# A block-causal attention with hashed experts: V fetched in two-token runs, interleaved key tiles, expert weights in 16 KB runs from batch 6 on

## The chip, the cores and the metric

One Trainium2 chip, of which the program uses one core. The metric is device microseconds of one execution, from the first to the last work of that core. Engines go by these names: PE (TensorE: PE for the matmul, PEld for the load of its stationary operand), DVE (VectorE), ACT (ScalarE), POOL (GpSimd), SP (SyncE, here only an issuer of transfers). "Lnnn" is a line of the kernel before.

## What is computed

Attention over 8 batches x 8 heads x 576 tokens x 64 dimensions in f32, causal in blocks of 64 tokens, then a mixture of experts in which a hash of the token's id, not its content, chooses one of 8 experts:

```python
scores = (1.0 / np.sqrt(D)) * np.matmul(q, k.transpose(0, 1, 3, 2))
mask = (pos[:, None] // 64) >= (pos[None, :] // 64)
attn = softmax(np.where(mask, scores, -1e9))          # rows
x = (attn @ v).transpose(0, 2, 1, 3).reshape(4608, 512)
e = token_ids * 2654435761 % 8
out[t] = np.maximum(x[t] @ w1[e[t]], 0.0) @ w2[e[t]]  # w1: 512x1024, w2: 1024x512, per expert
```

## The kernel before, in words

**Phase one, attention.** The order of the work is written out by hand: one loop over 32 head pairs (g = 4 b + pr: batch b, pair pr of two heads), plus two turns at the end, since PV lags two pairs behind. One turn issues, in this order: `S_chunk(g, 0)` and `S_chunk(g, 1)`, `PV(g-2, 0)`, the transposes `T_pair(g+1)` (and `T_rest` before a new batch), `S_chunk(g, 2)` (and `S_rest` in the first pair), `PV(g-2, 1)`; then the casts of the next batch and, between them, the loads of the one after that.

The first 512 tokens of a head are handled in four tiles of 128, the last 64 ("rest") by themselves. q and k are loaded with four neighbouring tokens per partition (1 KB runs; L106), the rest rows apart (L112). `cast_qk` turns them into bf16 on DVE (L169, L174), PE transposes them (L215), DVE copies the result to `qkT` (L220), and in this copy sorts the columns so that tile i holds tokens 128i to 128i+127. Within a tile the tokens stand in the order c, j for token 4j + c.

`S_chunk` (L245) makes scores with keys on partitions and queries on the free axis: three chunks of 2 heads x 512 columns into one of three `ps` buffers. `mm_pair` (L225) multiplies both heads, whose 64 dimensions lie on partitions 0 to 63 and 64 to 127 of the array. In a diagonal tile the upper 64 keys must not be seen by the lower 64 queries: two small matmuls (L239) of `maskk` and `maskq` add -30000 there. ACT takes the exponential of a whole chunk (L258) into `pt`. The rest rows get their own 64x64 scores (L266).

`PV` (L287) multiplies, for each head, 15 times (L299 x14, L304) into `O`, of which there is one buffer; a column of ones beside V gives the sum of each row. DVE takes the reciprocal (L309) and multiplies (L310) into the bf16 tile `xs`, 512 columns per token.

V is loaded with tokens matched to that order: 16 transfers of 64 KB per batch in runs of one token, 256 bytes (L122), and two for the rest (L128), all from SP's queue, in which q, k and V of batch after batch follow each other (`ld` has two buffers of each). `cast_v` on POOL (L179, L182) makes bf16 of it in `vx`, with two buffers.

`scatter_x(b-1)` on POOL (L323, in pair 1 of batch b) writes each token's row to the place in `x_dram` that `route()` has worked out (sorted by expert, 640 places per expert, on DVE during the first pairs of batch 0). Expert weights are cast from f32 to bf16 by the transfer itself, issued on POOL by `load_weights` (L471, L473) into one of three buffers: expert 0 in batch 3, expert 1 in batch 5, expert 2 in batch 7, always after that turn's scatter.

**Phase two, FFN.** When all rows are placed, SP issues the transposing load of expert 0's x (L553), the read of the rows' token numbers (L456), then the other experts' x. `stage_a` (L558) computes relu(x w1): per 128 columns of the hidden layer eight matmuls of 320 columns (L566), ACT does the relu (L571). `stage_b` (L576) multiplies by w2 (L581), DVE copies (L586), POOL scatters the rows to the output (L588). A loop over overflowing tiles follows (L614), which finds nothing to do here or little.

Of the kernel before, what the change touches and what calls it, by code (L numbers as in the profile page):

```python
# [14 lines left out]
ET = mybir.EngineType  # L15

# [4 lines left out]
NT = 4  # L21
# [13 lines left out]
def kernel(  # L35
# [27 lines left out]
    maskq = const.tile([P, 64], BF16, name="maskq")  # L63
# [14 lines left out]

    nc.vector.memset(maskk[:], 0.0)
    nc.vector.memset(maskq[:], 0.0)  # L80
    for m in range(2):
        nc.vector.memset(
            maskk[64 * m : 64 * m + 1, :].rearrange("p (c h j) -> p c h j", c=4, h=2)[:, :, 1, :], NEG)
        nc.vector.memset(maskq[64 * m : 64 * m + 1, :], 1.0)
# [32 lines left out]
    def load_v(b):  # L117
        vf = ld.tile([P, 36, D], F32, name="vf", tag="vf")
        vm = vf[:, 0:32, :].rearrange("p (h i) d -> p h i d", h=H)
        for i in range(NT):  # L120
            for c in range(4):
                nc.sync.dma_start(  # L122
                    vm[32 * c : 32 * c + 32, :, i, :],
                    v[b, :, 128 * i : 128 * i + 128, :].rearrange(
                        "h (j c) d -> c j h d", c=4)[c],
                )
        for m in range(2):
            nc.sync.dma_start(  # L128
                vf[64 * m : 64 * m + 64, 32:36, :],
                v[b, :, 512:576, :].rearrange("(r m) s d -> m s r d", m=2)[m],  # L130
            )
        loaded[b][2] = vf
# [3 lines left out]
    for z in range(2):  # L136
        vx = fix.tile([P, H, NT, D + 1], BF16, name=f"vx{z}")
        v4 = fix.tile([P, NP, 2, D + 1], BF16, name=f"v4{z}")
        nc.vector.memset(vx[:, :, :, D : D + 1], 1.0)
        nc.gpsimd.memset(v4[:], 0.0)  # L140
        for m in range(2):
            nc.vector.memset(v4[64 * m : 64 * m + 64, :, m, D : D + 1], 1.0)
        vexts.append((vx, v4))
# [32 lines left out]
    def cast_v(b):  # L176
        vf = loaded[b][2]
        vx, v4 = vexts[b % 2]
        nc.gpsimd.tensor_copy(  # L179
            vx[:, :, :, 0:D], vf[:, 0:32, :].rearrange("p (h i) d -> p h i d", h=H))  # L180
# [24 lines left out]
    def T_pair(g):  # L205
# [4 lines left out]
        tp = psT.tile([P, 8, P], BF16, name="tp", tag="tp")  # L210
        for w in range(2):
            src = casted[b][w]
            for c in range(4):
                s0 = (pr * 4 + c) * 2
                nc.tensor.transpose(  # L215
                    out=tp[:, 4 * w + c, :],
# [3 lines left out]
        nc.vector.tensor_copy(  # L220
            qk[:, pr, :, 0:512].rearrange("p w (i c j) -> p w c i j", i=4, c=4),
            tp[:].rearrange("p (w c) (i j) -> p w c i j", w=2, i=4),
        )

    def mm_pair(b, pr, ps, o0, i, q0, n):  # L225
        qk = qkTs[b]
        diag = q0 == 128 * i
        for m in range(2):
# [3 lines left out]
                lhsT=qk[rows, pr, 1, 128 * i : 128 * i + 128],  # L232
                rhs=qk[rows, pr, 0, q0 : q0 + n],
                start=True, stop=not diag,
            )
        if diag:
            for m in range(2):
                rows = slice(64 * m, 64 * m + 64)
                nc.tensor.matmul(  # L239
                    ps[:, m, o0 : o0 + 128].rearrange("p (c h j) -> p c h j", c=4, h=2)[:, :, 0, :],  # L240
                    lhsT=maskk[rows, :], rhs=maskq[rows, :].rearrange("p (c j) -> p c j", c=4),
                    start=False, stop=True,
                )

    def S_chunk(g, ch):  # L245
        b, pr = divmod(g, NP)
        ps = psS.tile([P, 2, 512], F32, name="ps", tag="ps")
        if ch == 0:
            mm_pair(b, pr, ps, 0, 0, 0, 512)
        elif ch == 1:  # L250
            mm_pair(b, pr, ps, 0, 1, 128, 448)
            mm_pair(b, pr, ps, 448, 0, 512, 64)
        else:
            mm_pair(b, pr, ps, 0, 2, 256, 320)
            mm_pair(b, pr, ps, 320, 3, 384, 192)
# [20 lines left out]
    def pt_off(i, q0):  # L276
        if i == 0:
            return q0 if q0 < 512 else 960
        if i == 1:
            return 512 + q0 - 128  # L280
        if i == 2:
            return 1024 + q0 - 256
        return 1344 + q0 - 384

    xss = {}

    def PV(g, m):  # L287
# [8 lines left out]
        for t in range(5):  # L296
            for i in range(min(t, NT - 1) + 1):
                o0 = m * PTW + pt_off(i, 128 * t)
                nc.tensor.matmul(  # L299
                    O[:, t, :], lhsT=pt[:, o0 : o0 + 128], rhs=vx[:, h, i, :],  # L300
                    start=(i == 0), stop=(i == t),
# [9 lines left out]
            out=xs[:, :, h * D : (h + 1) * D], in0=O[:, :, 0:D],  # L311
            in1=rs[:].to_broadcast([P, 5, D]), op=ALU.mult,
# [156 lines left out]
    def load_weights(e):  # L469
        w1b = wts.tile([P, DM // P, FF], BF16, name="w1b", tag="w1b")  # L470
        nc.gpsimd.dma_start(w1b[:], moe_w1[e].rearrange("(db p) f -> p db f", p=P))  # L471
        w2b = wts.tile([P, FF // P, DM], BF16, name="w2b", tag="w2b")
        nc.gpsimd.dma_start(w2b[:], moe_w2[e].rearrange("(fb p) o -> p fb o", p=P))  # L473
# [27 lines left out]
    for g in range(NPAIRS + 2):  # L501
# [29 lines left out]
        if pr == 1 and b >= 1:  # L531
            scatter_x(b - 1)
            if b == 3:
                load_weights(0)
            if b == 5:
                load_weights(1)
            if b == 7:
                load_weights(2)
# [19 lines left out]
    def stage_a(e):  # L558
# [3 lines left out]
        for ft in range(NFT):  # L562
            hp = psH.tile([P, 2, 512], F32, name="hp", tag="hp")
            for db in range(NKT):
                for t in range(2):
                    nc.tensor.matmul(  # L566
                        hp[:, t, 0:HC], lhsT=w1b[:, db, ft * P : (ft + 1) * P],
# [32 lines left out]
    load_x(1)  # L600
    hts = {}
# [12 lines left out]
    with tc.For_i(0, n_ov, 1) as j:  # L614
# [3 lines left out]
            w1b[:], moe_w1[bass.ds(eo, 1)].rearrange("e (db p) f -> p (e db) f", p=P))  # L618
        w2b = wts.tile([P, NFT, DM], BF16, name="w2b", tag="w2b")
        nc.gpsimd.dma_start(  # L620
            w2b[:], moe_w2[bass.ds(eo, 1)].rearrange("e (fb p) o -> p (e fb) o", p=P))
# [15 lines left out]
        for ft in range(NFT):  # L637
            hp = psY.tile([P, P], F32, name="hpo", tag="yp")
            for db in range(NKT):
                nc.tensor.matmul(hp[:], lhsT=w1b[:, db, ft * P : (ft + 1) * P], rhs=xt[:, db, :],  # L640
# [42 lines left out]
```

The softmax here doesn't subtract the row's maximum and nothing guards it: scores larger than these inputs give would overflow.

## Time and profile before

| What | us |
|---|---|
| median of 3 runs (lowest, highest) | 362.71 (361.36, 366.07) |
| the profiled execution / its span | 359.15 / 357.5 |
| attention: first scores, last O written out | 10.18, 190.2 |
| last scatter of x issued; first x transpose issued | 197.1; 200.97 |
| first and last FFN matmul's start | 205.64, 348 |
| busy: PE, ACT, DVE, POOL | 258.6, 143.5, 134.0, 126.5 |
| mean granted TensorE clock | 0.86 |

The profile cuts the span into 40 slices of 8.9 us and gives each engine's busy share in tenths; "PEclk" is the granted clock, "DMA" the share of the 16 DMA engines. The granted clock is 0.99 over the FFN phase and 0.68 to 0.92 over the batches of attention. Windows give busy microseconds (and instruction counts) in a stretch. In a list of waits the columns are: engine, line, what it waited for, microseconds in total, times, longest. In the order of time a line gives start, length, engine, line, tile written and read, count, and in brackets the idle time before it and who ended it. DMA volumes are counted as written, so a weight of 2 MB in f32 counts 1 MB. Other groups that matter: 96 exponentials of 1031 ns, 64 multiplies (L310) of 491, 8 casts of V (L179) of 1892, 16 of its rest (L182) of 399, 896 PV matmuls, 320 + 256 score and mask matmuls.

### The profile page before, as it was taken

Reading aid. Unit: us, or ns where it says so; the run is one execution under the profiler, and the core shown is the slowest. Engines: PE = TensorE matmul, PEld = TensorE weight load, DVE = VectorE, ACT = ScalarE, POOL = GpSimd, SP = SyncE. Lnnn points to the kernel's source line nnn. Section 1 sums busy time; section 2 is a strip of 40 time slices with the busy share of each in tenths; the row PEclk is TensorE's granted clock in tenths of the full one; section 3 lists DMA queues with packets and bytes.
Section 4 is the critical chain, followed back from the end, with each engine's and each line's share of the span. In section 5 each row is a group of like instructions: output and inputs, shape, how many; then the busy total and the mean of one; then the engine's idle time right before and its main releaser. Section 6 shows DMA issues by size and latency. Waiting matters only on the chain. (4 is left out here: it accounts for less than half of the span.)

```text
span 357.5 us, 6826 instructions
## 1 busy us (share of the span) xinstructions
PE 258.6 (72%) x2727; PEld 167.6 (47%) x2727; DVE 134.0 (37%) x311; ACT 143.5 (40%) x177; POOL 126.5 (35%) x154
## 2 busy tenths in 40 slices
PE   1425698496682776826961099999999989999990
PEld 0213475365462554624740067464747464646440
DVE  6528787454750756507551000213030303030330
ACT  1225397658291582913950046141515041415100
POOL 2040225726504556045374000343341606061451
PEclk9998599959586795865885579999999999999997
DMA  7678596879999989999149793469999998989231
GB/s 209 149 218 235 125 288 166 261 200 270 201 199 237 254 247 230 197 215 277 43 98 186 169 148 76 132 149 183 185 157 258 173 232 173 231 158 226 107 129 43
DMA packets 109152, 66.42 MB, mean 186 GB/s; under 512 B 75957, under 2 KB 101557, under 8 KB 109120
## 3 DMA queue, kind: packets, MB, share of 16 engines
q1 hardware_dynamic: 89984, 33.56, 40.7%
q0 software_dynamic: 17536, 31.24, 40.2%
q10 hardware_dynamic: 1600, 1.18, 1.1%
q8 instruction: 22, 0.36, 0.4%
q14 instruction: 10, 0.08, 0.1%
HBM read 61.92 MB, written 16.61 MB: 220 GB/s over the span
## 5 line engine op out<-in xcount | busy, mean ns | idle before, releaser
L258 ACT ACTIVATE pt<-ps 128x1024 bf16<-128x1024 f32 x96 | 92.1, 1031 | 81.1 <-PE ps L239 80.9
L571 ACT ACTIVATE hT<-hp 128x640 bf16<-128x640 f32 x64 | 45.0, 703 | 103.8 <-PE hp L566 103.8
L566 PE MATMUL hp<-xT,w1b 128*128 128x320 bf16 x512 | 72.7, 304 | 17.9 <-DMA xT<-x_dram 16.2
L299 PE MATMUL O<-vx,pt 128*128 128x65 bf16 x896 | 47.8, 214 | 42.5 <-DVE xs L310 27.4
L588 POOL DMA_INDIRECT out_dram<-ysb,perm x40 | 40.0, 999 | 104.5 <-DVE ysb L586 103.2
L581 PE MATMUL yp<-w2b,hT 128*128 128x512 bf16 x320 | 70.2, 379 | 0.0
L586 DVE COPY ysb<-yp 128x512 f32<-128x512 f32 x40 | 27.7, 691 | 112.1 <-PE yp L581 70.7
L566 PEld LDWEIGHTS <-w1b 128*128 128x128 bf16 x512 | 50.5, 99 | 40.3 <-issue 16.3
L299 PEld LDWEIGHTS <-pt 128*128 128x128 bf16 x896 | 39.4, 110 | 50.2 <-DVE xs L310 30.2
L323 POOL DMA_INDIRECT x_dram<-xs,slot_i x40 | 44.6, 1115 | 26.9 <-DVE xs L310 15.5
L581 PEld LDWEIGHTS <-hT 128*128 128x128 bf16 x320 | 31.3, 98 | 36.6
L179 POOL CAST vx<-vf 128x2048 bf16<-128x2048 f32 x8 | 15.1, 1892 | 90.5 <-DMA vf<-in_v_dram 79.3
L230 PE MATMUL ps<-qkT 64*128 64x512 bf16 (+4 forms) x320 | 44.5, 350 | 0.2
L310 DVE TENSOR_TENSOR xs<-O,rs 128x320 bf16<-128x320 f32 x64 | 31.4, 491 | 2.2
L230 PEld LDWEIGHTS <-qkT 64*128 64x128 bf16 x320 | 18.4, 106 | 20.0 <-issue 7.5
L239 PE MATMUL ps<-maskq,maskk 64*128 64x64 bf16 x256 | 25.5, 213 | 0.0
L309 DVE RECIPROCAL rs<-O 128x5 f32<-128x5 f32 x64 | 12.3, 192 | 31.1 <-PE O L304 30.6
L220 DVE COPY qkT<-tp 128x1024 bf16<-128x1024 bf16 x32 | 21.8, 682 | 4.1 <-PE tp L215 3.8
L169 DVE CAST qb<-qf 128x2048 bf16<-128x2048 f32 (+2 forms) x9 | 10.7, 1194 | 32.1 <-DMA qf<-in_q_dram 32.1
L215 PE MATMUL tp<-identbf,qb 128*128 128x128 bf16 x128 | 15.1, 253 | 9.5 <-DVE qb L169 9.5
L215 PE MATMUL tp<-identbf,kb 128*128 128x128 bf16 x128 | 14.8, 249 | 4.3 <-DVE kb L169 4.3
L215 PEld LDWEIGHTS <-qb 128*128 128x128 bf16 x128 | 9.6, 115 | 9.7 <-DVE qb L169 9.6
(99 smaller groups left out, 135.1 us busy)
## 6 DMA issues: line engine op xcount, KB each, us to landing
vf<-in_v_dram SPq DMA_DIRECT2D x144, 64.0 KB
w1b<-in_moe_w_dram POOLq DMA_DIRECT2D x8, 1024.0 KB, 8.0
w2b<-in_moe_w_dram POOLq DMA_DIRECT2D x8, 1024.0 KB, 14.8
qf<-in_q_dram SPq DMA_DIRECT2D x7, 1024.0 KB
kf<-in_k_dram SPq DMA_DIRECT2D x7, 1024.0 KB
x_dram<-zx SPq DMA_DIRECT2D x8, 136.0 KB
qf<-in_q_dram SPq DMA_DIRECT2D x16, 64.0 KB
kf<-in_k_dram SPq DMA_DIRECT2D x14, 64.0 KB
```

The lines of the kernel that those rows point to most:

```text
L215: nc.tensor.transpose(out=tp[:, 4 * w + c, :], in_=src[:, s0 : s0 + 2, :].rearrange("p a d -> p (a d)"), identity=identbf[:],)
L230: nc.tensor.matmul(ps[:, m, o0 : o0 + n], lhsT=qk[rows, pr, 1, 128 * i : 128 * i + 128], rhs=qk[rows, pr, 0, q0 : q0 + n], start=True, sto ...
L239: nc.tensor.matmul(ps[:, m, o0 : o0 + 128].rearrange("p (c h j) -> p c h j", c=4, h=2)[:, :, 0, :], lhsT=maskk[rows, :], rhs=maskq[rows, : ...
L258: nc.scalar.activation(ptv[:, :, 512 * ch : 512 * ch + 512], ps[:], ACT.Exp, scale=SCALE)
L299: nc.tensor.matmul(O[:, t, :], lhsT=pt[:, o0 : o0 + 128], rhs=vx[:, h, i, :], start=(i == 0), stop=(i == t),)
L310: nc.vector.tensor_tensor(out=xs[:, :, h * D : (h + 1) * D], in0=O[:, :, 0:D], in1=rs[:].to_broadcast([P, 5, D]), op=ALU.mult,)
L323: ins = nc.gpsimd.indirect_dma_start(out=x_dram[:, :], out_offset=bass.IndirectOffsetOnAxis(ap=slot_i[0:n, i, b : b + 1], axis=0), in_=xs[ ...
L566: nc.tensor.matmul(hp[:, t, 0:HC], lhsT=w1b[:, db, ft * P : (ft + 1) * P], rhs=xT[:, db, t * HC : (t + 1) * HC], start=(db == 0), stop=(db ...
L571: nc.scalar.activation(hT[:, ft, :].rearrange("p (t n) -> p t n", t=2), hp[:, :, 0:HC], ACT.Relu)
L581: nc.tensor.matmul(yp[:], lhsT=hT[:, ft, tt * P : (tt + 1) * P], rhs=w2b[:, ft, :], start=(ft == 0), stop=(ft == NFT - 1),)
L586: nc.vector.tensor_copy(ysb[:], yp[:])
L588: ins = nc.gpsimd.indirect_dma_start(out=out[:, :], out_offset=bass.IndirectOffsetOnAxis(ap=perm3[:, gg : gg + 1], axis=0), in_=ysb[:], in ...
```

## The change

- **V**: 8 transfers of 128 KB per batch instead of 16 of 64 KB. A run is two neighbouring tokens, 512 bytes. The 256 tokens 256r to 256r+255 now form two key tiles: even and odd tokens (slot 2r + c), instead of two tiles of 128 consecutive tokens.
- **Scores**: queries keep their four tiles. Key tiles of 256r.. now matter in part for a query tile: for query tiles 0 and 2 only the lower half of two key tiles is seen. These halves are put together into one 128-row piece by `mm_c`, with 64x64 pieces. The masks change with it, and a pair has 30 score and mask matmuls instead of 18. `T_pair` writes the transposes directly in the wanted order, so the copy to `qkT` is straight. The exponentials keep their number and size, and PV its 15 matmuls a head, from the columns that the table `PVS` lists.
- **cast_v**: `vx` has six slots instead of four; two more POOL copies bring the two lower halves together.
- **Weights**: row p of the array holds w1's rows 4p to 4p+3 and w2's rows 8p to 8p+7: 16 KB in one run for either. So the columns of x are permuted when `PV` writes `xs` (reading `O` with a step of four), and w1's stationary operand takes every eighth column.
- **When**: expert 0 in the first pair of batch 6 (ahead of the scatter of batch 5, which is issued a turn later), expert 1 in pair 1 of batch 7, expert 2 behind the first two x transposes in the program, so on POOL right after the last scatter.

```diff
     def load_v(b):
-        vm = vf[:, 0:32, :].rearrange("p (h i) d -> p h i d", h=H)
-        for i in range(NT):
-            for c in range(4):
-                nc.sync.dma_start(
-                    vm[32 * c : 32 * c + 32, :, i, :],
-                    v[b, :, 128 * i : 128 * i + 128, :].rearrange("h (j c) d -> c j h d", c=4)[c])
+        vm = vf[:, 0:32, :].rearrange("p (h r c) d -> p h r (c d)", h=H, r=2)
+        for r in range(2):
+            for hf in range(2):
+                for u in range(2):
+                    p0 = 64 * hf + 32 * u
+                    t0 = 256 * r + 128 * hf
+                    nc.sync.dma_start(
+                        vm[p0 : p0 + 32, :, r, :],
+                        v[b, :, t0 : t0 + 128, :].rearrange("h (j u c) d -> u j h (c d)", u=2, c=2)[u])
     def cast_v(b):
-        nc.gpsimd.tensor_copy(vx[:, :, :, 0:D], vf[:, 0:32, :].rearrange("p (h i) d -> p h i d", h=H))
+        vm = vf[:, 0:32, :].rearrange("p (h s) d -> p h s d", h=H)
+        nc.gpsimd.tensor_copy(vx[:, :, 0:4, 0:D], vm)
+        nc.gpsimd.tensor_copy(vx[0:64, :, 4:6, 0:D], vm[0:64, :, 0::2, :])
+        nc.gpsimd.tensor_copy(vx[64:128, :, 4:6, 0:D], vm[0:64, :, 1::2, :])
     def T_pair(g):
...
-                nc.tensor.transpose(out=tp[:, 4 * w + c, :], in_=..., identity=identbf[:])
-        nc.vector.tensor_copy(qk[:, pr, :, 0:512].rearrange("p w (i c j) -> p w c i j", i=4, c=4),
-                              tp[:].rearrange("p (w c) (i j) -> p w c i j", w=2, i=4))
+                if w == 0:
+                    o = tp[:, 0, :].rearrange("p (i c j) -> p c i j", i=4, c=4)[:, c]
+                else:
+                    o = tp[:, 1, :].rearrange("p (r x h u j) -> p u x r h j", r=2, x=2, h=2, u=2)[:, c // 2, c % 2]
+                nc.tensor.transpose(out=o, in_=..., identity=identbf[:])
+        nc.vector.tensor_copy(qk[:, pr, :, 0:512], tp[:])
+    def mm_c(b, pr, ps, o0, r):
+        for x in range(2):
+            for m in range(2):
+                rows = slice(64 * m, 64 * m + 64)
+                nc.tensor.matmul(ps[64 * x : 64 * x + 64, m, o0 : o0 + 128],
+                    lhsT=qk[rows, pr, 1, 256 * r + 128 * x : 256 * r + 128 * x + 64],
+                    rhs=qk[rows, pr, 0, 256 * r : 256 * r + 128], start=False, stop=False)
     def S_chunk(g, ch):
-        if ch == 0:
-            mm_pair(b, pr, ps, 0, 0, 0, 512)
-        elif ch == 1:
-            mm_pair(b, pr, ps, 0, 1, 128, 448)
-            mm_pair(b, pr, ps, 448, 0, 512, 64)
+        if ch < 2:
+            mm_pair(b, pr, ps, 0, ch, 128, 448, first=True)
+            mm_pair(b, pr, ps, 448, 3 - ch, 512, 64)
+            mm_mask(ps, 0, False, 1, last=True)
         else:
-            mm_pair(b, pr, ps, 0, 2, 256, 320)
-            mm_pair(b, pr, ps, 320, 3, 384, 192)
+            mm_pair(b, pr, ps, 256, 2, 384, 128, first=True)
+            mm_pair(b, pr, ps, 384, 3, 384, 128)
+            mm_mask(ps, 256, False, 2)
+            mm_c(b, pr, ps, 0, 0)
+            mm_c(b, pr, ps, 128, 1)
+            mm_mask(ps, 0, True, 2, last=True)
     def PV(g, m):
...
-            out=xs[:, :, h * D : (h + 1) * D], in0=O[:, :, 0:D],
-            in1=rs[:].to_broadcast([P, 5, D]), op=ALU.mult,
+            out=xs[:, :, 0:DM].rearrange("p t (d h k) -> p h t d k", d=4, h=H)[:, h],
+            in0=O[:, :, 0:D].rearrange("p t (k d) -> p t d k", d=4),
+            in1=rs[:, :, :, None].to_broadcast([P, 5, 4, D // 4]), op=ALU.mult,
     def load_weights(e):
-        nc.gpsimd.dma_start(w1b[:], moe_w1[e].rearrange("(db p) f -> p db f", p=P))
+        nc.gpsimd.dma_start(w1b[:], moe_w1[e].rearrange("(p db) f -> p db f", p=P))
-        nc.gpsimd.dma_start(w2b[:], moe_w2[e].rearrange("(fb p) o -> p fb o", p=P))
+        nc.gpsimd.dma_start(w2b[:], moe_w2[e].rearrange("(p fb) o -> p fb o", p=P))
     # the loop over pairs
         if pr == 1 and b >= 1:
             scatter_x(b - 1)
-            if b == 3: load_weights(0)
-            if b == 5: load_weights(1)
-            if b == 7: load_weights(2)
+            if b == 7: load_weights(1)
+        if pr == 0 and b == 6: load_weights(0)
     def stage_a(e):
-                        hp[:, t, 0:HC], lhsT=w1b[:, db, ft * P : (ft + 1) * P],
+                        hp[:, t, 0:HC], lhsT=w1b[:, db, ft::NFT],
     # ahead of the FFN loop
     load_x(0)
     read_perm()
     load_x(1)
+    load_weights(2)
```

## The prediction

> **What bounds the kernel now.** I read the page's slices first, then windows cut at each batch, then SP's queue in order of time, the DMA queues in single windows, the waits, and last the few microseconds in which nothing is short.
>
> The slices, and the busy times of one batch without and one with a weight fetch, and of the FFN phase (sum columns: PE, PEld, DVE, ACT, POOL, granted clock, DMA share, GB/s):
>
> ```profile
> PE   1425698496682776826961099999999989999990
> DMA  7678596879999989999149793469999998989231
> 72.90:92.66 19.76, 14.70 (x238) 10.92 (x236) 11.08 (x27) 12.17 (x15) 9.38 (x11) 0.76 0.88 238
> 92.66:115.48 22.82, 14.18 (x217) 10.48 (x213) 8.35 (x21) 11.25 (x13) 6.22 (x7) 0.72 0.99 198
> 205.64:348.70 143.06, 141.25 (x832) 81.81 (x832) 27.58 (x43) 44.99 (x64) 47.62 (x49) 0.99 0.85 170
> ```
>
> The FFN phase is TensorE's (141.25 of 143.06 us). Attention, from 10 to 190 us, is not: no engine passes 17 us of 20 while the DMA share is 0.88 to 0.99. What paces the transfers is SP's own queue:
>
> ```profile
> 62.48 0.56 SPq L106 DMA_DIRECT2D qf<-in_q_dram  x1
> 65.03 3.21 SPq L112 DMA_DIRECT2D kf<-in_k_dram  x2
> 68.34 10.91 SPq L122 DMA_DIRECT2D vf<-in_v_dram  x16
> 79.29 1.26 SPq L128 DMA_DIRECT2D vf<-in_v_dram  x2
> 80.65 0.55 SPq L106 DMA_DIRECT2D qf<-in_q_dram  x1
> 88.35 16.56 SPq L122 DMA_DIRECT2D vf<-in_v_dram  x16
> ```
>
> SP issues without a pause, q, k, then V, batch after batch; from one batch's q to the next 19.83, 18.17 and 16.86 us pass, and 17.06 for the last batch: 17.98 on average. Sixteen V issues take 8.27 us where nothing is before them (32.97 to 41.28: 0.517 us each), and in that stretch the DMA engines are only half busy (first line below; columns: packets, MB, share). With a weight fetch in flight (92 to 104 us; second and third line) POOL's queue has 80% and SP's 19%, and the two batches that hold fetches take 29.02 and 28.07 us, 10.6 more than the others.
>
> ```profile
> q1 hardware_dynamic: 4693, 1.38, 54.0%
> ...
> q0 software_dynamic: 1131, 1.80, 80.2%
> q1 hardware_dynamic: 1431, 0.35, 18.6%
> ```
>
> The waits say the same, the longest from POOL and DVE for V and q:
>
> ```profile
> POOL vx L179 <- DMA vf<-in_v_dram: 79.3, 6, 18.6
> DVE qb L169 <- DMA qf<-in_q_dram: 32.1, 7, 10.7
> PEld L299 <- DVE xs L310: 30.2, 30, 4.4
> PE hp L566 <- DMA xT<-x_dram: 16.2, 1, 16.2
> ```
>
> The third is the next bound. Where all data is there, a head's O buffer (one only) makes a chain: PV, reciprocal, multiply, next PV.
>
> ```profile
> 182.18 0.62 PE L299 MATMUL O<-vx,pt 128*128 128x65 bf16 x14 [0.43 <-DVE xs L310]
> 182.87 0.20 DVE L309 RECIPROCAL rs<-O 128x5 f32<-128x5 f32 x1 [0.74 <-PE O L304]
> 183.10 0.49 DVE L310 TENSOR_TENSOR xs<-O,rs 128x320 bf16<-128x320 f32 x1
> 183.65 0.62 PE L299 MATMUL O<-vx,pt 128*128 128x65 bf16 x14 [0.82 <-DVE xs L310]
> ```
>
> That is 1.46 us a head, 2.93 a pair. Pairs begin at 173.86, 176.80 and 179.85, so an unhindered batch takes some 13.1 us (4 x 3.0, 0.4 for the rest rows' scores, 0.7 for their transposes). Data costs 18 where the engines need 13.
>
> **The change part by part.** All is summed against the profiled execution, 359.15 us (span 357.5); the median of three runs is 362.71, 1.0% above it.
>
> V: 16 issues of 64 KB become 8 of 128 KB, 512 B in a run instead of 256. An issue does not follow bytes in this trace: 1 MB of q takes 0.55 us, 64 KB of the rest rows 0.61. So 8 x 0.517 = 4.1 us leave SP's period: 17.98 to 13.9. The data must fit below that: V's packets run at 132 / 0.54 = 244 GB/s of full share, q and k's 1 KB ones near 360; 512 B lies between, some 300 GB/s, 3.5 us for 1.05 MB against 4.1 of issue. It fits.
>
> Scores: per pair 30 matmuls instead of 18 (320 + 256 in all become 960). Streamed columns go from 3584 to 4608, in row pairs that run together; a mask of 64 columns starts the next matmul 0.03 us later (178.91 to 178.94), and the eight 64x64 matmuls of the rest rows take 0.31 us at 46.60, of which 0.19 is one. The third chunk, now 0.29 us, becomes 0.35 to 0.55; the first two lose as much. PE has 0.2 to 0.4 us of waits a pair to pay from, so 0 to 0.25 us a pair, 0 to 1 us a batch. ACT's exponentials stay at 0.92 us apart, 2.95 a pair. [...]
>
> The normalising multiply (L310) reads O with every fourth f32. Nothing in the trace reads PSUM so. [...] Above: L405, which reads SBUF at every 40th f32, takes 758 ns for 320 elements where L433 takes 410 for 256 side by side, so 1.9 ns an element instead of 1.05: +0.27 us. It sits in the O chain, twice a pair: up to 0.54 x 4 = 2.2 us a batch. PSUM and a step of four are nearer to the present L310 than to L405; I take +0.05 (0.4 a batch) and keep both ends.
>
> Cast of V: two more POOL copies of 64x1024. From 1892 ns for 2048 and 399 for 256 elements, 0.83 ns each and 186 fixed: 1.04 us each, 2.1 a batch. POOL has 6 to 9 of 20 us in use; behind the casts stand the scatter issues, which wait for xs anyway. At the start POOL's iota, for which DVE waits 4.9 us at 23.19, is behind V's first cast: V lands 4.1 earlier, is cast 2.1 later: -2.0 us. Transposes and the qkT copy keep counts and sizes (682 ns): 0; the larger mask tile too.
>
> So a batch needs 13.9 of SP and 13.1 + 0.4 + 0.5 = 14.0 of the O chain and PE; two bounds so near each other do not mesh fully, and I take 14.5 (13.4 to 15.6). The loop from pair 4 (43.64) to the last two pairs' PV (182.18) took 138.5; 7 x 14.5 = 101.5: -37.0 us. Both former fetches are in this.
>
> Weights: expert 0 is now issued on POOL at the first pair of batch 6, ahead of the scatter of batch 5 and just while V(7), and perhaps q(7), come in. A fetch took 10.6 us of such a batch. V(7) is first read two pairs into batch 7, some 20 us on: +1.5 us taken, 0 to 10.6. Expert 1 stands where expert 2 stood (batch 7, pair 1), as far ahead of the last scatter: 0. Expert 2 is now behind the last scatter on POOL (ended 197.1) and runs beside the first x transpose (issued 200.97, first matmul 205.64), the list of rows and the second transpose. With SP's queue at 19% for those 10 us the first transpose ends little before the fetch (about 209) or just after, at 211 to 212: +6.0 us, 0 to 10.6. Experts 1 and 2 are used 9 and 26 us later: covered.
>
> FFN: in 16 KB runs the fetch reads the same bytes; it writes 195 GB/s of bf16, so reads 390 of f32, more than the 360 of q and k: no gain taken. TensorE waited 4.9 us for w1b, so -4.9 to 0. Weight loads of the first product now step 16 bytes. A stage's eight matmuls take 1.086 us (relu starts at 211.06 and 212.15), 135.8 ns each; contiguous loads pass every 30 ns where little else binds (PV: 14 in 0.49 us with 0.10 for one). With L405's factor of 1.8 they would be 54 ns: still hidden: 0. The bound above is rival one. [...]
>
> Sum: 359.15 - 2.0 - 37.0 + 1.5 + 6.0 = 327.7; with the 1.0% of the median, **331 us**.
>
> **The rivals.** One, on the other side: the strided weight load comes out from under its matmul. Loss: (s - 135.8 ns) x 512, for a spacing s. [...] At s = 198 ns all 32 us of gain are gone; at eight times 30 = 240 ns it is +53: 384 us.
> Two: the O chain or PE becomes the bound at 16 us a batch (L310 at its upper end, 2.2, and the whole 1 us of matmuls): 7 x 1.5 = +10.5: 341 to 342. For it: L405, and O waits already 30 us; against it: the multiply's present rate.
> Three: a V issue costs by its bytes, so the run length does nothing: 18 us a batch, 7 x 3.5 = +24.5, the start's 2.0 lost, and a full collision with expert 0, +9: 366.5, no change. Against it: 1 MB in 0.55 us.
>
> **How the numbers follow.** Forecast 0.63, two 0.18, three 0.06, one 0.13. The forecast's own range is 315 to 346 (batch at 13.4 to 15.6: -8 and +8; collisions -7.5 and, in part, +7). With rival two it reaches 314 to 352; one and three, 0.19, are left out. About 2% is what a measurement of this kernel can tell from no change. Faster: 0.63 + 0.18 = 0.81. Same: three and a part of one (s near 198), 0.06 + 0.03 = 0.09. Slower: 0.10.
>
> **What would show it.** SP: 8 V issues in some 4 us when unhindered, q to q in about 14; if 8, rival three. L310 near 0.5 us, or 0.76 for rival two. Relu starts of the first expert 1.09 us apart, else rival one. The first FFN matmul some 15 us after the last xs (now 15.4) would mean the transpose lost nothing; I expect 21. No fetch in batches 3 to 5; one beside V(7), and a wait for it if I am wrong there. What would make all of it wrong: a fetch with longer runs that shuts SP's queue out for longer than its bytes, or pairs that stop for PE at 3.5 us.

## The result, and the profile after

| | before | after |
|---|---|---|
| median of the runs shown together (lowest, highest), us | 364.39 (361.36, 367.59) | 395.6 (395.45, 396.13) |
| the profiled execution / its span | 359.15 / 357.5 | 395.62 / 394.0 |
| last multiply of attention | 190.2 | 216.4 |
| from there to the first FFN matmul | 15.4 | 22.3 |
| first to last FFN matmul | 143.0 | 140.8 |
| from there to the end of the span | 8.9 | 14.5 |
| mean granted TensorE clock | 0.86 | 0.81 |

The ratio is 1.089 [1.080, 1.098]: the changed kernel is slower, where 331 us and "faster" were forecast. Of the 36.5 us between the two profiled executions, 26.1 lie in attention, 6.9 ahead of the first FFN matmul, 5.6 behind the last one, and the FFN gives 2.1 back.

Page of after, slices of 9.85 us; then windows of after: two batches, and the FFN (columns as before: length, PE, PEld, DVE, ACT, POOL, granted clock, DMA share, GB/s).

```profile
PE   1353764938569294783945007999999999999950
DMA  7999998859656591461048499547979999895230
```

```profile
102.20:126.10 23.90, 15.45 (x288) 11.50 (x286) 12.87 (x28) 12.27 (x15) 10.81 (x12) 0.71 0.67 176
126.10:150.00 23.90, 15.45 (x288) 11.52 (x286) 12.89 (x28) 12.27 (x15) 10.82 (x12) 0.71 0.67 176
238.67:380.00 141.33, 140.42 (x824) 101.25 (x832) 28.00 (x43) 45.06 (x64) 44.77 (x49) 0.99 0.81 172
```

The trains of scatters that mark the batches start at 101.69, 125.61 and 149.51, so 23.92 and 23.90 us apart, with the same busy times: nothing random paces them. No engine is over 15.5 of 23.9, and the DMA share, 0.88 to 0.99 before, is 0.67. The bound of before is gone and something slower has come.

SP in order of time, from one batch to the next, and the first transposing load:

```profile
78.34 0.39 SPq L110 DMA_DIRECT2D qf<-in_q_dram  x1
...
90.83 5.51 SPq L129 DMA_DIRECT2D vf<-in_v_dram  x8
96.38 1.26 SPq L135 DMA_DIRECT2D vf<-in_v_dram  x2
102.28 0.39 SPq L110 DMA_DIRECT2D qf<-in_q_dram  x1
...
225.03 11.44 SPq L581 DMA_TRANSPOSE xT<-x_dram  x1
```

V is what the change meant: 8 issues in 5.5 us in place of 16 in 8 to 19. But SP now stands still between 97.6 and 102.3, as it does in every batch: it no longer sets the pace. What does, stands in the few microseconds after 102 (DVE, POOL, PE of after):

```profile
102.79 0.68 DVE L234 COPY qkT<-tp 128x1024 bf16<-128x1024 bf16 x1
108.97 0.20 DVE L338 RECIPROCAL rs<-O 128x5 f32<-128x5 f32 x1 [5.49 <-remote]
109.19 0.49 DVE L339 TENSOR_TENSOR xs<-O,rs 128x320 bf16<-128x320 f32 x1
109.60 2.29 DVE L176 CAST kb<-kf 128x2048 bf16<-128x2048 f32 x1
```

```profile
101.69 1.21 POOL L353 DMA_INDIRECT x_dram<-xs,slot_i  x1 [11.64 <-DVE xs L339]
...
107.01 0.90 POOL L353 DMA_INDIRECT x_dram<-xs,slot_i  x1 [0.30 <-issue]
107.91 1.92 POOL L187 CAST vx<-vf 128x2048 bf16<-128x2048 f32 x1
```

```profile
103.39 0.19 PE L333 MATMUL O<-v,pt 128*128 128x65 bf16 x1
...
104.53 0.21 PE L265 MATMUL ps<-maskq,maskk 64*128 64x64 bf16 x2
109.74 0.95 PE L328 MATMUL O<-vx,pt 128*128 128x65 bf16 x14 [5.00 <-DVE xs L339]
```

The reciprocal needs O. O's last matmul ended at 103.58. The reciprocal began at 108.97, DVE idle all the while. That POOL's scatters block DVE itself is unlikely: DVE's copy at 102.79, beside them, takes its usual 0.68 us. "Remote" is the profile's word where it finds no instruction whose end released the wait. The trace also records every change of a semaphore; for TensorE's own they stand against the matmuls that signal like this:

```
ends of signalling matmuls:  102.13  102.70  103.55  103.58  103.95  104.74          110.75
changes recorded:            102.15  105.28  108.94, 109.02, 109.09 (one is missing)  110.76
```

At 102.13 and 110.75 the signal follows its matmul by 0.01 to 0.02 us, which is the rule in all traces here (median 0.014). Between, the matmuls run (their starts are recorded, their ends modelled) and their signals come up to 5.4 us late, in one burst. There POOL issues the five scatters of x back to back (101.69 to 107.91, the "train"). Matched to the next change recorded, which understates it, 34 of 335 signals of after come over 0.4 us late, all beside a train; two more, in the FFN, have no change of their own in the record. The profile shown of before has none, though it has the same trains. The waits sum it up, with the FFN's wait for the transpose:

```profile
DVE rs L338 <- remote: 35.8, 7, 5.9
...
PE hp L594 <- DMA xT<-x_dram: 23.1, 1, 23.1
...
ACT pt L289 <- remote: 17.9, 6, 3.7
```

One wait of some 5 us on DVE in each of seven batches, and one on ACT beside it.

### The profile page after: what moved, and what is told of

Read it like the earlier page. It is cut to its first block, busy times and chain, and to the rows that moved or that the text cites. A ratio compares the mean times of both kernels' runs of the same rounds, so it can differ in the third digit from the quotient of the medians.

```text
span 394.0 us, 7530 instructions
## 1 busy us (share of the span) xinstructions
PE 269.1 (68%) x3103; PEld 196.6 (50%) x3111; DVE 149.0 (38%) x311; ACT 144.6 (37%) x177; POOL 137.5 (35%) x170
## 3 DMA queue, kind: packets, MB, share of 16 engines
q1 hardware_dynamic: 72576, 33.56, 37.5%
## 5 line engine op out<-in xcount | busy, mean ns | idle before, releaser
L289 ACT ACTIVATE pt<-ps 128x1024 bf16<-128x1024 f32 x96 | 93.1, 1026 | 105.3 <-PE ps L265 83.8
L594 PEld LDWEIGHTS <-w1b 128*128 128x128 bf16 x512 | 70.0, 145 | 25.9 <-issue 23.2
L353 POOL DMA_INDIRECT x_dram<-xs,slot_i x40 | 39.7, 992 | 106.1 <-DVE xs L339 96.4
L328 PEld LDWEIGHTS <-pt 128*128 128x128 bf16 x896 | 40.0, 112 | 50.2 <-DVE xs L339 37.5
L241 PE MATMUL ps<-qkT 64*128 64x64 bf16 (+2 forms) x384 | 38.7, 299 | 2.4 <-issue 1.2
L265 PE MATMUL ps<-maskq,maskk 64*128 64x64 bf16 (+2 forms) x320 | 31.0, 236 | 0.4 <-issue 0.4
L229 PE MATMUL tp<-identbf,kb 128*128 128x128 bf16 x128 | 16.4, 268 | 13.3 <-DVE kb L176 13.3
L229 PE MATMUL tp<-identbf,qb 128*128 128x128 bf16 x128 | 16.2, 267 | 8.4 <-DVE qb L176 8.4
L265 PEld LDWEIGHTS <-maskk 64*128 64x128 bf16 (+1 forms) x320 | 16.5, 123 | 9.9 <-issue 6.5
L176 DVE CAST kb<-kf 128x2048 bf16<-128x2048 f32 (+2 forms) x9 | 20.4, 2271 | 0.0
L241 PEld LDWEIGHTS <-qkT 64*128 64x128 bf16 x384 | 13.5, 102 | 10.5 <-issue 6.5
```

Source lines behind the costliest of these rows:

```text
L229: nc.tensor.transpose(out=o, in_=src[:, s0 : s0 + 2, :].rearrange("p a d -> p (a d)"), identity=identbf[:],)
L241: nc.tensor.matmul(ps[:, m, o0 : o0 + n], lhsT=qk[rows, pr, 1, 128 * kt : 128 * kt + 128], rhs=qk[rows, pr, 0, q0 : q0 + n], start=first, ...
L265: nc.tensor.matmul(ps[prt, m, o0 : o0 + 128 * n].rearrange("p (t h j) -> p t h j", h=2, j=16)[:, :, 0, :], lhsT=maskk[rows, 64:128] if c e ...
L289: nc.scalar.activation(ptv[:, :, 512 * ch : 512 * ch + 512], ps[:], ACT.Exp, scale=SCALE)
L328: nc.tensor.matmul(O[:, t, :], lhsT=pt[:, m * PTW + o0 : m * PTW + o0 + 128], rhs=vx[:, h, i, :], start=(n == 0), stop=(n == t),)
L353: ins = nc.gpsimd.indirect_dma_start(out=x_dram[:, :], out_offset=bass.IndirectOffsetOnAxis(ap=slot_i[0:n, i, b : b + 1], axis=0), in_=xs[ ...
```

## The experiments

Two theories. **Held signals**: while POOL issues a train of scatters, TensorE's signals are held up; in the kernel before, the waits for q and V covered that. **Narrow pieces**: the 64x64 matmuls of the scores (L253, L265) do it, by themselves or by what they leave in TensorE's queue. A third, tried later: the longer casts of V behind the train.

**The narrow pieces, taken out of after.** A third copy on DVE makes a key tile of the two halves, so that full-width matmuls do.

```diff
+        nc.vector.tensor_copy(kcs[b][:, pr]..., tp[:, 1, :]...[:, :, :, 0, :])
     def mm_c(b, pr, ps, o0, r):
-        for x in range(2):
-            for m in range(2):
-                nc.tensor.matmul(ps[64 * x : 64 * x + 64, m, o0 : o0 + 128], ...
+        for m in range(2):
+            nc.tensor.matmul(ps[:, m, o0 : o0 + 128], lhsT=kcs[b][rows, pr, r, :], ...
```

> The changed kernel with the 64x64 score pieces of the third chunk taken out: the 128 keys of each piece are copied side by side into a tile of their own (one more 128x256 copy a pair on DVE, about 0.29 us by the row for such a copy), so that the score and its mask are full 128-column matmuls, 6 fewer a pair. Theory 'narrow pieces' (a 64-column matmul that runs while GpSimd issues the x scatter has its completion held until the scatter's issues are over): the waits put down to remote, 35.8 us on DVE and 17.9 on ACT, fall below 4 us, q to q goes from 23.92 to 18 to 19.5 us, and the time to 355 to 368. Rival 'scatter and casts' (whatever runs beside the scatter is held, and the casts of V right behind it, now that V is there, hold DVE): the waits stay at 5.5 us a batch and q to q at 24 to 25: 395 to 405.

377.4 us, ratio to before 1.032 [1.024, 1.041]. Remote waits fall to 16.5 (DVE) and 13.7 us (ACT) but stay, and a batch (from the last multiply of one to that of the next) still takes 18.0 to 24.0 us. Neither theory's number: a part of the time goes with the pieces, or with the time at which the train falls, which this edit moves too.

**Half-width pieces put into before.** Scores of the last key tile as two 64-column halves.

```diff
+        if i == 3:
+            for x in range(2):
+                for m in range(2):
+                    nc.tensor.matmul(ps[64 * x : 64 * x + 64, m, o0 : o0 + n], ...
```

> The kernel before with only one edit: the scores of the fourth key tile and their mask in the third chunk are made as two 64-column halves (8 matmuls of 64x64 in place of 4 of 64x128 a pair), the same result. Theory 'narrow pieces': waits put down to remote appear on DVE and ACT during the x scatters, 2 to 6 us each, 10 to 40 us in all; the time goes up by 0 to 25 us, 364 to 390, as the loads of V cover part of it. Rival 'scatter and casts': nothing of the kind appears, 360 to 371.

364.4 us, 1.002 [0.996, 1.009]: no cost. It has remote waits too, 12.2 and 12.4 us, so that before itself had to be looked at a second time.

**The weight half alone** (w1, w2 in 16 KB runs, x permuted, the new times) on before's V and scores.

```diff
-        nc.gpsimd.dma_start(w1b[:], moe_w1[e].rearrange("(db p) f -> p db f", p=P))
+        nc.gpsimd.dma_start(w1b[:], moe_w1[e].rearrange("(p db) f -> p db f", p=P))
...
+        if pr == 0 and b == 6:
+            load_weights(0)
```

> The kernel before with the weights' half of the change alone: 16 KB runs, x and FFN rows permuted, fetches from batch 6 on; V as before. By the prediction's terms: two fetches leave batches 3 and 5 (10.6 us each), expert 0 costs 1.5 to 10.6 in batch 6, expert 2 beside the first x transpose 6 to 10.6: 347 to 360, most likely 353, and no remote waits under either theory. If the gap before the first FFN matmul grows to 23 us as in the changed kernel, it belongs to this half.

367.0 us, 1.006 [1.003, 1.010]. Remote waits 13.3 and 9.0 with no narrow piece for the scores of the main tiles. The first FFN matmul comes 22.8 us after the last multiply.

**The V half alone**, with the weights as before.

```diff
-            if b == 7:
+            if b == 3:
+                load_weights(0)
+            if b == 5:
...
-                        hp[:, t, 0:HC], lhsT=w1b[:, db, ft::NFT],
+                        hp[:, t, 0:HC], lhsT=w1b[:, db, ft * P : (ft + 1) * P],
```

> The changed kernel with the weights' half undone: V in two-token runs with the new key tiles, weights in their old runs at batches 3, 5 and 7. If the stall belongs to the V half, under both theories, the remote waits stay (about 5.5 us a batch), q to q stays near 23.9 with the fetches hidden in the idle DMA time, the gap before the first FFN matmul returns to 15 us: 385 to 392. If it is the two halves together that make it, 345 to 360.

370.2 us, 1.022 [1.014, 1.030]. Remote waits 26.3 and 15.9. The V half alone, which should have brought the gain, loses, and 370.2 lies in neither of the ranges expected; 1.006 and 1.022 make 1.028, both together 1.089.

**Before once more**, unchanged, to see whether its held signals are the edits' doing.

> The kernel before, unchanged, profiled once more beside the others. Theory 'narrow pieces' is already in doubt: the weights' half alone, which has none, showed 13 us of remote waits. Theory 'hold' (the five scatter instructions in a row on GpSimd hold back the completions that TensorE signals, in any version, and the change only took away the wait for data under which this lay): this execution, too, shows updates of TensorE's semaphore that come over 0.4 us late during most of the seven x scatters, and remote waits of some 10 us, at 359 to 369 us in all. Rival 'made by the change': none comes late, as in the profile shown of before.

363.0 us. DVE and the waits of this run:

```profile
89.79 0.68 DVE L220 COPY qkT<-tp 128x1024 bf16<-128x1024 bf16 x1
93.03 0.20 DVE L309 RECIPROCAL rs<-O 128x5 f32<-128x5 f32 x1 [2.56 <-remote]
```

```profile
DVE rs L309 <- remote: 7.7, 4, 2.6
```

So before has them as well in this execution, over 30 late signals, though the profile shown has none. DVE waits 2.6 us here at most, not 5.5. The time is that of the other runs, so these holds cost little here; that the waits for q and V cover them is inferred, not shown. The narrow pieces are not needed for it.

**The train taken apart in after.** The five scatters are paced, by a dependency on the last multiply issued, at the ends of pairs 1, 2 and 3 and twice in the next batch's first pair; the casts of V stand between them.

```diff
+            tc.add_manual_dep(ins.ins, pace[0].ins.name, SYNC, reason="pace")
...
+        if b >= 1 and pr == 1:
+            scatter_x(b - 1, 0, 1 if b < B else 5)
+        if c and pr == 1:
+            cast_v(b + 1, (0,))
+        if b >= 1 and pr == 2:
+            scatter_x(b - 1, 1, 2)
...
```

> The changed kernel with the five scatter instructions of a batch spread over five points (ends of pairs 1, 2 and 3, middle and end of the next pair 0), each made to wait for the multiply of that point, and the casts of V put between them. Theory 'hold' by a train of back-to-back scatters: the remote waits (35.8 us on DVE, 17.9 on ACT) fall below 15 in all, the period from 23.9 to 18 to 20 us, the time to 358 to 372. Rival 'each scatter costs its own hold': the total of the waits stays, 388 to 398. Rival 'the casts of V on GpSimd beside DVE's cast of k': the waits go but q to q stays above 21.5, 378 to 388.

361.3 us, 0.9996 [0.993, 1.006]: 34 us less than after by an edit that moves the same bytes by the same instructions. Remote waits of DVE:

```profile
DVE rs L342 <- remote: 0.8, 1, 0.8
```

That is 0.8 in place of 35.8; ACT's fall from 17.9 to 2.7, and TensorE has three of its own, 6.0 in all. The holds are not gone, only short: some 20 signals still come over 0.4 us late, up to 2.0, all beside a scatter. Where a stretch of the record has as many changes as signals, so that they can be matched in order, the longest delay beside one scatter alone is 0.9 us, beside two back to back 2.0, beside a train of five 5.7 (in after, and in all kernels on the chip of these runs and on the second one below). The rival "each scatter costs its own hold" is right in that, but holds this short are seldom waited for. A new wait, 12.6 us in all, came in: the multiply waits for a scatter to land, since with two xs buffers the last scatter is now a batch late; and the 22 us ahead of the FFN are still there.

**The third fetch moved back** in after, to the last pair of batch 7.

```diff
+        if pr == 3 and b == 7:
+            load_weights(2)
     load_x(1)
-    load_weights(2)
```

> The changed kernel with the fetch of expert 2 taken back ahead of the last batch's scatter (issued in pair 3 of batch 7 instead of behind the first x transposes). Theory: the fetch shares the DMA engines with the first x transpose, whose issue took 11.44 us where it took 2.43 before: the gap from the last multiply to the first FFN matmul goes from 23 to 15 or 16 us, all else equal: 386 to 389. Rival: the gap is the transpose's own, 394 to 397.

383.6 us, 1.065 [1.045, 1.085]. The first transposing load takes 2.63 us instead of 11.44, but starts only at 221.56: the last scatter was issued from 206.91 on, and POOL's DMA queue, into which two fetches had gone at 194.69 to 196.91, then had 99.5% of the DMA engines (205 to 212). Its attention is also 10 us shorter than that of after (the last reciprocal at 205.4, not 215.6) though the edit touches nothing ahead of batch 7; so the holds are not the same in every run of nearly the same program.

**All three: full-width pieces, paced scatters, third fetch early.**

> The changed kernel with all three: full-width score pieces, the scatter spread, expert 2 fetched ahead of the last scatter. Theory 'hold': period 16 to 18 us and the gap of 15: 335 to 352, faster than both kernels. If the period stays at 20 or more, what limits it is neither the hold nor the narrow pieces: 365 or more.

360.2 us, 0.986 [0.975, 0.997]; between the two ranges expected; no remote wait at all, though 25 signals still come 0.4 to 1.75 us late beside the scatters; the stretch ahead of the FFN still 22.1.

**The casts of V ahead of the train** in after (issued in pair 1 before the scatters). This run and those that follow, up to the weight half in its parts, were made on a second chip.

```diff
+            if pr == 1:
+                cast_v(b + 1)
-            if pr == 3:
-                cast_v(b + 1)
```

> The changed kernel with the casts of V moved ahead of the scatter on GpSimd's queue; the five scatter instructions stay a train. It tells apart what spreading the scatter left together. Theory 'train': the remote waits stay, 25 to 55 us in all, some 6 us later in each batch, 380 to 400. Rival 'the casts that stand right behind the scatter': they fall below 10 us, 358 to 370.

382.9 us, 1.057 [1.050, 1.064]:

```profile
DVE rs L338 <- remote: 25.6, 6, 4.4
```

The train holds the signals with no cast behind it. The third theory falls; what the casts did to DVE moved with them (qb's nine casts now take 17.4 us and kb's 10.7; in after kb's took 20.4 and qb's 10.7).

**Before with paced scatters** and three xs buffers.

> The kernel before with the scatter spread over the same five points, and three buffers for xs instead of two. Theory: its train of scatters lies under the wait for data, so taking it apart gains little, 352 to 364; the comparison without the train is then the changed kernel spread (361.3) against this. If the train cost the kernel before as much as the changed one, 330 to 345.

355.1 us, 0.983 [0.974, 0.991]. Remote waits 3.2 and 1.4. In before, pacing and the third xs buffer together gain 1.7%; what either gains alone was not run.

**After with full-width pieces, paced scatters, three xs buffers, the three fetches in batches 4, 5, 6.**

> The changed kernel with full-width score pieces, the scatter spread, three buffers for xs (the multiply waited 9.9 us for the scatter's landing in the run with all three edits) and the fetches of experts 0, 1 and 2 in batches 4, 5 and 6, so that none stands in the queue ahead of the last scatter or beside the first x transpose. Theory: the gap from the last multiply to the first FFN matmul goes from 23 to 15.4 us, the waits of the multiply go, period 16.5 to 18: 338 to 350. If the gap stays at 22, it is not the fetch: 350 to 356.

354.5 us, 0.980 [0.974, 0.986]: the stretch ahead of the FFN closes as expected, the batches do not. Batches with a fetch 19.8 to 21.8 us, without one 15.7 to 18.0; 13.2 us ahead of the FFN.

**The same with the narrow pieces put back.**

> The kernel of the run beside it (spread, three buffers, early fetches) with the 64x64 score pieces of the change put back. Theory 'narrow pieces cost PE and ACT time of their own': 3 to 8 us slower than with full-width pieces, as the attention of the two spread runs so far ended 4.7 us apart. Rival 'they cost nothing, and the copy that replaces them costs DVE 9 us': the same or up to 5 us faster.

353.8 us, 0.976 [0.970, 0.983]: with the train apart the narrow pieces cost nothing that these runs can tell. They do not make the loss by themselves, so the second theory falls; why taking them out beside the train gained 18 us (the first run) stays open.

**The V half alone, paced**, three xs buffers, weights as before.

> The V half alone (weights, x order and fetches as in the kernel before) with the scatter spread and three buffers for xs. Theory 'the V half does what was predicted once nothing is held': batches without a fetch at 15 to 16.5 us, those with one at 20 to 22, 335 to 346, against 355.1 of the kernel before spread alike. Rival 'its own additions (pieces, masks, two more casts) take back what the issues give': 350 to 360.

350.5 us, 0.973 [0.961, 0.985]; against before with the same pacing (0.983 [0.974, 0.991]) only 1% less, and the intervals overlap: that the V half gains anything is not shown. Batches take 15.2 to 22.1 us.

**The third fetch held** in after, by dependencies, until the first two transposing loads are in.

```diff
+        for r in behind:
+            tc.add_manual_dep(i1.ins, r.ins.name, SYNC, reason="behind the first x")
...
-    load_x(1)
-    load_weights(2)
+    first.append(load_x(1))
+    load_weights(2, first)
```

> The changed kernel with one edit: the fetch of expert 2 waits until the first two x transposes have landed. Theory 'the fetch beside the transpose': the first transpose's issue goes from 11.44 to about 2.5 us, the gap from the last multiply to the first FFN matmul from 23 to 14 or 15 us, and the FFN phase is no longer for it (expert 2 is needed some 26 us on): 378 to 389, of which 8 to 9 us are the gap. Rival 'the transpose itself': gap 22 or 23, 388 to 397.

378.9 us, 1.054 [1.038, 1.071]. SP's and PE's lines:

```profile
215.92 2.43 SPq L584 DMA_TRANSPOSE xT<-x_dram  x1
```

```profile
220.57 19.85 PE L598 MATMUL hp<-xT,w1b 128*128 128x320 bf16 x128 [14.08 <-DMA xT<-x_dram]
```

2.43 us for the load that took 11.44 beside the fetch; 13.3 us from the last multiply to the first FFN matmul, not 22.3. That is 9.0 us for the collision; the rest of the difference to after is again a shorter attention.

**After, paced, three xs buffers, third fetch held.**

> The changed kernel with the scatter spread, three buffers for xs and the fetch of expert 2 held as in the run beside it; score pieces as in the change, experts 0 and 1 fetched where the change put them (batches 6 and 7). Theory: no fetch meets a load of V or q before batch 6, so batches 1 to 5 at 15 to 18 us, gap 14: 338 to 350. If it stays at 353 to 356, as the two kernels with early fetches, another limit stands behind the train.

346.4 us, 0.963 [0.946, 0.981]: less than either kernel, and 32.5 us less than with the train and two xs buffers, measured beside it. Against before paced alike (0.983) it is 2% less, with intervals that overlap a little. Its windows, batches 5 and 6:

```profile
110.60:125.40 14.80, 12.19 (x288) 9.25 (x288) 10.85 (x27) 12.27 (x15) 10.15 (x10) 1.00 0.96 273
125.40:142.70 17.30, 12.80 (x294) 9.42 (x298) 11.41 (x28) 12.46 (x15) 11.70 (x12) 1.00 0.40 114
```

14.80 us for the same 288 matmuls that took 23.90, at a granted clock of 1.00 in place of 0.71 (15.45 us busy become 12.19), with the DMA engines at 0.96. It is the shortest batch: from last multiply to last multiply the seven take 14.8 to 20.2 us, 17.2 on average. Two others, of 15.6 and 20.0 us, come at nearly the same clock, 0.78 and 0.74; why some need 20 is not settled. Some 30 signals still come over 0.4 us late in this kernel.

**The weight half in its three parts**, on before: w1's runs (with x permuted), w2's runs (with the strided weight load), the times alone. They are for the end, 5.6 us longer in every kernel with the weight half (14.2 to 14.5 us from the last FFN matmul, 8.9 to 9.5 in those without), of which 4.8 are POOL's last DRAIN.

> Kernel of before with w1 alone in 16 KB runs (and the columns of x permuted for it, the multiply reading O with a step of four); w2, the weight loads of the first product and the times of the fetches as before. The question is the end: from the end of the last FFN matmul to the end of the span pass 8.9 to 9.5 us in every kernel without the weight half and 14.2 to 14.5 in every kernel with it, of which 4.8 are the last DRAIN on POOL (3.09 against 7.91 us) and 1.2 an instruction before it (0.9 against 2.1). If this follows the runs of the fetches, some of it shows here: a DRAIN above 3.1 us, 5.5 if the halves add. If it follows the times of the fetches: 3.09 and a tail of 8.9. The multiply stays at 491 ns.

> Kernel of before with w2 alone in 16 KB runs, w1's stationary operand taking every eighth column for it; w1, x and the times as before. If the end follows the runs of the fetches: a last DRAIN between 3.1 and 7.9 us, 5.5 if the halves add. If it follows the times: 3.09 us and a tail of 8.9. Weight loads of the first product 145 ns instead of 99, still hidden, relu starts 1.09 us apart.

> Kernel of before with only the times of the three first fetches as in the kernel after (batch 6, batch 7, behind the first two loads of x), all layouts as before. If the end follows the times: a last DRAIN of 7.9 us and a tail of 14.5; if it follows the runs: 3.09 and 8.9. For the term of the third fetch: the stretch from the last multiply to the first FFN matmul should be about 22, as in the kernels in which the third fetch goes beside the first transposing load, if it is the time that counts and not the run length; about 13 if it is the run length.

Single runs: 353.1, 356.8 and 358.8 us, before 356.5 beside them. The end is 8.3, 7.4 and 8.9 us, the DRAIN 2.5, under 0.9 and 3.1. No part alone lengthens it; together (the weight half alone, further up) they do, and the times are not needed for it: the two kernels with the fetches in batches 4, 5 and 6 end in 14.2 us as well. What is left is w1's and w2's long runs together, which were not run with the old times. Both accounts fail and the cause of these 5.6 us stays open. The other question is answered: with the times alone and old, short runs the first transposing load takes

```profile
191.16 9.36 SPq L551 DMA_TRANSPOSE xT<-x_dram  x1
```

and 24.8 us pass from the last multiply to the first FFN matmul; with w1's or w2's long runs alone 2.48 and 2.50, and 15.7 and 15.8 us. When the fetch is issued counts; long runs are not needed for it.

These three ran on a third chip, and have one or two late signals where before itself, half-width pieces or the weight half had over 30, with the same trains. So the hold is not made by the program alone. The kernel after was not run in that session.

The four corners, as ratios to before of the same session:

| scatters of x | before | weight half | V half | both | both, third fetch held |
|---|---|---|---|---|---|
| one train | 1 | 1.006 | 1.022 | 1.089 | 1.054 |
| paced, three xs buffers | 0.983 | not run | 0.973 | 1.000 (two xs buffers) | 0.963 |

## Why the prediction was wrong

**The step that failed** is the batch: "a batch needs 13.9 of SP and 13.1 + 0.4 + 0.5 = 14.0 of the O chain and PE ... I take 14.5", and in it the one sentence that dismissed POOL: "behind the casts stand the scatter issues, which wait for xs anyway". Forecast 7 x 14.5 us; measured 23.9 in the regular batches. The list of bounds lacked one: beside the train TensorE's signals come late, and DVE, ACT and then TensorE wait. The prediction did not ask what the scatters would cost once the waits for q (32.1 us) and V (79.3 us) were gone, and the profile that it read has no late signal that could have told it; a second profile of the same kernel has over 30. That the train of scatters costs these waits is shown by pacing it (35.8 us of remote waits to 0.8, 395.6 to 361.3; on the second chip 378.9 to 346.4, there with a third xs buffer). That in before the waits for q and V cover it is inferred. Why the signals are held, and why DVE waits longer for them in after (5.5 us) than in before (2.6), is not known.

The train is not all of the miss. With it apart and the fetch held, the kernel still takes 346.4, 15 us over the forecast, though the +6.0 for the fetch is saved: one batch comes down to 14.80, but the seven average 17.2 in place of 14.5, some 19 us, and the end is 5.6 longer. So 14.5 was too low as a price for the two bounds named as well, and what makes the difference stays open. One reading under it was off: SP did not issue "without a pause"; between 40 and 172 us of before, 11.3 us in seven waits of V's issues (L122) are put down to the landing of k.

Point by point:

- **V's issues**, 4.1 us for eight forecast, 4.9 to 6.4 measured behind the first eight (0.61 to 0.79 each): a little low, and of no account, since SP waits for the buffers. Rival three, cost by bytes (8.3), did not happen.
- **Start**, -2.0: the first reciprocal of after is at 32.2, that of before at 33.6 in the profile shown and 32.1 in the second. No gain shown.
- **Scores**, 0 to 1 us a batch: not contradicted (0.976 against 0.980 with and without the narrow pieces, the train apart); the added matmuls as a whole were not taken out by themselves.
- **Multiply with a step of four**, +0.05 taken, up to +0.27: neither. No run shows the 0.05, nor the 0.4 us a batch that the sum holds for it. Groups of after (busy, mean ns of one, idle ahead):

```profile
L594 PEld LDWEIGHTS <-w1b 128*128 128x128 bf16 x512 | 70.0, 145 | 25.9 <-issue 23.2
...
L339 DVE TENSOR_TENSOR xs<-O,rs 128x320 bf16<-128x320 f32 x64 | 31.5, 492 | 2.2
```

  492 ns, before 491.
- **Weight loads by 16 bytes**: 145 ns against 99 mean, hidden; the FFN's matmuls take 140.42 us busy, before 141.25. Rival one, which had 0.13, is refuted.
- **Casts of V**, 2.1 us a batch, put at nothing: they do not hold the signals (382.9 with the casts first), but kb's cast beside them takes 2.27 to 4.46 us in six batches instead of 1.21 to 1.38, 20.4 us in all against 10.9, just behind the hold. Why it is slower there, no run tells.
- **Expert 0 in batch 6**, +1.5: batch 6 of after took 23.9 us, as the others; nothing to see behind the hold. In the kernel with fetches in batches 4 to 6 those batches took 19.8 to 21.8 us, the others 15.7 to 18.0.
- **Third fetch beside the first transposing load**, +6.0 (0 to 10.6): 9.0, by the held fetch. The mechanism was right and the size within its bounds. In the stretch 223 to 237 of after, POOL's queue has 80.4% of the DMA engines and SP's 14.5%, where the prediction reckoned with 19.
- **The end**: not in the sum at all; +5.6.

The sum with the measured sizes: 359.15 + 26.1 (for -37.5) + 6.9 (for +6.0) - 2.1 + 5.6 = 395.6. Rival two's "16 us a batch" is not what happened either; the last sentence, "pairs that stop for PE at 3.5 us", came nearest: of the four steps of a regular batch of after, from one copy into qkT to the next, the one that holds the train takes 10.7 us, the one behind it, with the rest rows and the casts, 6.1, and the two others 3.6 each.

## What to carry to other kernels

When a change takes a long wait away, list what else happened during that wait on every engine, the issuers of transfers too, and ask of each what it would cost in the open; a train of five indirect transfers from POOL cost the kernel before some 1.7% (the gain of a third xs buffer counted in), and the changed one some 34 us. Spread such a train over the batch before speeding up the loads: with a third xs buffer, and the third fetch out of the way of the transposing load, that turned a loss of 8.9% into a gain of 3.7%. One profile without an effect does not show that the kernel is free of it: look at a second, on another chip if there is one.

## What the runs showed of the hardware

- TensorE's completion signals, 0.014 us after the matmul at the median, come up to 5.7 us late beside five indirect transfers that GpSimd issues in 6.2 us, up to 2.0 beside two, up to 0.9 beside one; matmuls go on starting meanwhile (in after at 103.39 and 104.53, between signals at 102.15 and 105.28), and in the trains of after the held signals then come mostly 0.03 to 0.08 us apart. In the profile shown of before no train does this (no signal over 0.024 us late), and on the third chip nearly none (one or two late signals a run). In the FFN the same instruction writes 40 sets of rows to the output, 1.0 us each, and no signal recorded beside these is over 0.02 us late. So such a transfer is not enough by itself; what else it takes, no run tells.
- The granted clock changes from batch to batch: 0.71 in after's regular batches, 1.00 in the shortest batch of the paced kernel, with 15.45 and 12.19 us for the same 288 matmuls. It is no simple mark of the hold: two other batches of the paced kernel have 0.78 and 0.74.
- The first transposing load of x takes 2.43 to 2.68 us, but 9.36 beside a cast fetch of weights in short runs, and 11.44 to 11.93 beside one in long runs.
- The last DRAIN on POOL takes 7.91 us to the hundredth in every kernel with both weight layouts, whatever the times of the fetches, 3.09 in those with neither, 2.52 with w1's runs alone, under 0.9 with w2's alone. No run explains it.
